# Rearranging the opening of a Fourier and mixture kernel on one NeuronCore: where mu is turned, who makes the angles, when the next butterflies run

## The chip, the cores and the metric

The kernel runs on one core of a Trainium2 chip. The metric is the device time of one execution in microseconds (us); medians are given with the lowest and highest run. The span, which the profile measures from the first to the last instruction, is about 1.8 us shorter.

## The reference, cut to what matters

```python
X = np.fft.fft(np.fft.fft(x, axis=1), axis=2).real          # x: 8 x 3072 x 256
x_prev = shifted by one row along the sequence, zero first
xk = mu_k * X + (1.0 - mu_k) * x_prev
xr = mu_r * X + (1.0 - mu_r) * x_prev
k = np.maximum(xk @ w_k, 0.0)                                # 256 -> 1024
v = k * k @ w_v                                              # 1024 -> 256
out = 1.0 / (1.0 + np.exp(-(xr @ w_r))) * v
```

## The kernel before

The transform is done by matmuls in stages. Stage A works on x (for later batches on sums and differences of its columns, the butterflies), stages D and C follow with tables of sines, and VectorE turns C's result `pq` into halves `y`, differences `d` and mixes `x`. Then come the K, V and R products of each of 48 chunks. The batches are interwoven: while the chunks of one batch are multiplied, the next batch is transformed. At the start there is nothing to interweave, so the opening is a chain. TensorE's products go to PSUM tiles `psW` and `psV`, and ScalarE or VectorE evacuates them.

```python
def mu_turn():                       # mu from a row onto the partitions, by TensorE
    ps = ps_v()
    for a in range(2):
        for i in range(2):
            nc.tensor.matmul(out=ps[:, c:c + 1], lhsT=mu_p[:, a, i], rhs=one, ...)
    V.tensor_copy(out=mu_f.rearrange("p a i -> p (a i)"), in_=ps[:, 0:4])
...
def loads():                         # all issued by GpSimd, in this order
    ... gathers of w_k ...
    nc.gpsimd.dma_start(out=wv_sb, in_=moe_w_v...)
    load_xh(1, 0)                    # x of batch 1, first half
    ... gathers of w_r ...
    load_xh(1, 1)                    # second half
...
    a_sum(0, 1, 4)                   # main sequence
    mu_turn()
    m_ends()                         # the end terms of the first table
    eo_rest()
    a_sum(0, 1, 8)
    a_sum(0, 1, 12, "V", 2)
    a_sum(0, 1, 14, "A", 2)
    m_angles(NS1, NSL)               # second table, on VectorE
    keep_busy(2)                     # two filler products on zeros
    d_half(0, 0, ps_v(), "A")
    ...
```

After that the work is put into numbered steps, one K step of a chunk each; `at(step, f, ...)` places it.

Of the kernel before, what the change touches and what calls it, by code (L numbers as in the profile page):

```python
# [9 lines left out]
FP32 = mybir.dt.float32  # L10
# [3 lines left out]
AF = mybir.ActivationFunctionType  # L14
ALU = mybir.AluOpType

TWO_PI = 2.0 * math.pi
MAGIC = 12582912.0


def _v(ap, extra_offset, free_dims):
    new_ap = [list(ap.ap[0])] + [[s, c] for (s, c) in free_dims]
    return dataclasses.replace(ap, offset=ap.offset + extra_offset, ap=new_ap)
# [12 lines left out]
def kernel(  # L36
# [10 lines left out]
    nc = tc.nc  # L47
# [3 lines left out]
    P = 128  # L51
    N1, R = 48, 64
    NSL = 27
    GU = 386
    NS1 = 17

    const = ctx.enter_context(tc.tile_pool(name="const", bufs=1))
# [16 lines left out]
    def ps_w():  # L74
        return ps_slot("W", 3, 1024)

    def ps_v():
        return ps_slot("V", 2, 512)
# [23 lines left out]
    def load_part(b, h, q0, nq):  # L102

        nc.gpsimd.dma_start(out=xh_t[b, h][:, q0:q0 + nq],  # L104
                            in_=x_r[b, :, 16 * h + q0:16 * h + q0 + nq, :])

    def load_xh(b, h):
        xh_t[b, h] = xh_pool.tile([96, 16, 256], FP16, name="xh")
        load_part(b, h, 0, 16)

    V = nc.vector
# [24 lines left out]
    def keep_busy(n):  # L136

        ps = ps_v()
        for _ in range(n):
            nc.tensor.matmul(out=ps[:, 0:512], lhsT=zeros[:, 0:P], rhs=zeros, start=True, stop=True)  # L140
# [14 lines left out]
                                 in_=_v(mu_row, f0, [(256, 2), (step, n)]), func=AF.Copy)  # L155

    def mu_turn():
        ps = ps_v()
        for a in range(2):
            for i in range(2):  # L160
                c = 2 * a + i
                nc.tensor.matmul(out=ps[:, c:c + 1], lhsT=mu_p[:, a, i], rhs=one,
                                 start=True, stop=True)
        V.tensor_copy(out=mu_f.rearrange("p a i -> p (a i)"), in_=ps[:, 0:4])
# [17 lines left out]
    for c in range(2):  # L182
        nc.gpsimd.tensor_scalar(out=ueo[:, :, c], in0=veo_i, scalar1=pd_f,
                                scalar2=(0.5 + 0.25 * c) * TURN, op0=ALU.mult, op1=ALU.add)
    load_part(0, 1, 0, 8)
    kst_i = const.tile([P, NSL + 64], INT32)
    nc.gpsimd.iota(kst_i[:, 0:NSL], pattern=[[1, NSL]], base=-1, channel_multiplier=0)
    nc.gpsimd.iota(kst_i[:, NSL:NSL + 64], pattern=[[1, 64]], base=0, channel_multiplier=0)
# [126 lines left out]
    def m_angles(s0, s1):  # L315
        V.tensor_tensor(out=ang[:, s0:s1], in0=_v(ast, s0, [(1, s1 - s0), (0, 64)]),
                        in1=_v(ast, NSL, [(0, s1 - s0), (1, 64)]), op=ALU.add)

    def m_wrap(s0, s1):
        V.tensor_scalar(out=ang[:, s0:s1], in0=ang[:, s0:s1], scalar1=TURN - 1,  # L320
                        scalar2=None, op0=ALU.bitwise_and)

    def m_sine(s0, s1):
        nc.scalar.activation(out=m1[:, s0:s1], in_=ang[:, s0:s1], func=AF.Sin, bias=m_pi,
                             scale=TWO_PI / TURN)
# [9 lines left out]
    def m_ends():  # L335


        for n, m in enumerate((m1, m2)):
            V.tensor_scalar(out=m[hi64, 0], in0=m[hi64, 0], scalar1=-1.0, scalar2=None,
                            op0=ALU.mult)  # L340
            V.tensor_copy(out=mz[lo64, n], in_=m[lo64, 1])
            V.memset(m[:, 0, 0:1], 0.0)

    def m_last():

# [18 lines left out]
    def loads():  # L364
        for a in range(2):
            next(row_part)
            gather(wk_sb[0][a], moe_w_k, a)
        nc.gpsimd.dma_start(out=wv_sb, in_=moe_w_v.rearrange("(fc p) v -> p fc v", p=128))
        load_xh(1, 0)
        for a in range(2):  # L370
            gather(wr_sb[0][a], moe_w_r, a)
        load_xh(1, 1)
        next(row_part)
        for a in range(2):
            gather(wk_sb[1][a], moe_w_k, 2 + a)
        for a in range(2):
            gather(wr_sb[1][a], moe_w_r, 2 + a)
# [92 lines left out]
    def c_item(b, s0, n, eng="A"):  # L470

        if s0 == 0:
            y_t[b] = y_pool.tile([P, 2, NSL, 64], FP16, name="y")
            y_t[b, "pq"] = y_pool.tile([P, 2, NSL, 64], FP16, name="pq")
        pq = y_t[b, "pq"]
        ps = ps_w()
        for i in range(n):
            sl = s0 + i
            u = {-1: 1, 24: 0, 25: 23}.get(sl - 1, sl - 1)
            for o, col, m, first, last in ((0, 128, m1, True, True), (512, 0, m2, True, b > 0),  # L480
                                           (512, 256, m1, False, True))[:2 if b else 3]:
                nc.tensor.matmul(out=ps[:, o + 64 * i:o + 64 * i + 64],  # L482
                                 lhsT=g_all[:, u, col:col + 128],
                                 rhs=m[:, sl] if sl != 1 else mz[:, 0 if m is m1 else 1],
                                 start=first, stop=last)
        if b and s0 + n == NSL:
            for k in range(2):
                nc.tensor.matmul(out=ps[:, 448:512], lhsT=u128[:, k],
                                 rhs=(m1, m2)[k][:, 1], start=(k == 0), stop=(k == 1))
        evac(pq[:, :, s0:s0 + n, :], _v(ps, 0, [(512, 2), (64, n), (1, 64)]), eng)  # L490
        if b and s0 + n == NSL:
            y_t[b, "f"] = f = y_pool.tile([NSL, 64], FP16, name="f")
            nc.scalar.activation(out=f, in_=ps[0:NSL, 448:512], func=AF.Copy)
# [16 lines left out]
    def halves(b, lo, hi, hs=(0, 1)):  # L510

        pq = y_t[b, "pq"]
        for h in hs:
            V.tensor_tensor(out=y_t[b][:, h, lo:hi], in0=pq[:, 0, lo:hi], in1=pq[:, 1, lo:hi],
                            op=ALU.subtract if h else ALU.add)

    def diff(b, lo, hi, hs=(0, 1)):
        if (lo, hs[0]) == (0, 0):
            x_t[b] = mix_pool.tile([P, 2, 26, 64], FP16, name="d")
        y = y_t[b]  # L520
        a0, a1 = hs[0], hs[-1] + 1
        V.tensor_tensor(out=x_t[b][:, a0:a1, lo:hi], in0=y[:, a0:a1, lo + 1:hi + 1],
                        in1=y[:, a0:a1, lo:hi], op=ALU.subtract)
# [65 lines left out]
                             in_=st["k", ds].rearrange("p (f t) -> p f t", f=2),  # L589
                             func=AF.Relu, bias=0.0, scale=0.25)  # L590

    def square(c, ds):
        r = st["rl"][:, 2 * ds - 2:2 * ds + 2]
        V.tensor_tensor(out=k2_t[c][:, 2 * ds - 2:2 * ds + 2], in0=r, in1=r, op=ALU.mult)  # L594

    def r_item(c):
        b, m, i = c
# [47 lines left out]
    m_swap(0, NS1)  # L645
    a_sum(0, 1, 0, "V")
    a_sum(0, 1, 4)
    mu_turn()
    m_ends()
    eo_rest()  # L650
    a_sum(0, 1, 8)
    a_sum(0, 1, 12, "V", 2)
    a_sum(0, 1, 14, "A", 2)
    m_angles(NS1, NSL)
    keep_busy(2)
    d_half(0, 0, ps_v(), "A")
    d_half(0, 2, ps_v(), "V")
    d_half(0, 4, ps_w(), "A")
    d_half(0, 6, ps_w(), "V")
    m_wrap(NS1, NSL)  # L660
    c_item(0, 0, 5)
    c_item(0, 5, 4)
    d_item(0, 2)
# [4 lines left out]
    work = {}  # L668

    def at(step, f, *args):  # L670
        work.setdefault((step, "x" if f in (a_item, a_sum, d_item, c_item, r_item, m_sine, d_pair) else "w"),
                        []).append((f, args))

    def mirrored_mu():

        for a in range(2):
            nc.gpsimd.tensor_copy(out=mu_m[:, a], in_=mu_f[:, 1 - a])
        nc.gpsimd.tensor_copy(out=mu_m[0:1], in_=mu_f[0:1])  # L678

    chunks = [(b, m, i) for b in range(B) for m in range(2) for i in range(3)]  # L680
    nk = 4 * len(chunks)
# [5 lines left out]
    for step, (c, tb) in v_steps.items():  # L687
        if c == chunks[-1] and tb >= 2:
            o_steps[step] = [(c, tb, 1)]
        elif tb % 2:  # L690
            o_steps[step + (step == LAG)] = [(c, tb, 2)]
    for lo, hi in ((0, 4), (4, 8)):
        halves(0, lo + (lo > 0), hi + 1)
        diff(0, lo, hi)
        mix_part(0, 0, lo, hi)
        if lo == 0:
            keep_busy(4)
            c_item(0, 9, 8)
            k_products(chunks[0], 0, 0, 256)
            k_products(chunks[0], 1, 0, 256)  # L700
    for n, c in enumerate(chunks):
        at(4 * n + (4, 5, 6)[(n < 3) + (n == 0)], r_item, c)


    at(0, halves, 0, 9, 17)
    at(1, m_sine, NS1, NSL)
    at(0, diff, 0, 8, 16)
    at(1, mix_part, 0, 0, 8, 16)
    at(2, m_swap, NS1, NSL)
    at(2, m_last)  # L710
    at(3, d_pair, 0, 16)
    at(4, d_item, 0, 5)
    at(4, mix_part, 0, 1, 0, 8)
    at(5, c_item, 0, 17, 8)
    at(5, halves, 0, 17, 25)
    at(5, diff, 0, 16, 24)
    at(5, mix_part, 0, 0, 16, 24)
    at(5, plain_128)
    at(5, mirrored_mu)
    at(6, a_sum, 1, 0, 0)  # L720
    at(6, a_sum, 1, 0, 4)
    at(6, mix_part, 0, 1, 8, 16)
    at(7, butterfly, 1, 1, 0)
    at(7, a_sum, 1, 0, 8)
    at(7, a_sum, 1, 0, 12)
    at(8, c_item, 0, 25, 2)
    at(8, load_xh, 2, 0)
    at(8, butterfly, 1, 1, 1)
    at(8, halves, 0, 25, 27)
    at(8, diff, 0, 24, 26)  # L730
    at(9, mix, 0, 0, 1, 0)
# [48 lines left out]
    for step in range(nk + LAG):  # L780
        if step < nk:
            k_piece(chunks[step // 4], step % 4)
        due(step, "x")
        v = v_steps.get(step)
        if v:
            v_tile(*v)
        due(step, "w")
        for v in o_steps.get(step, ()):
            v_out(*v)
        if step < nk and step % 2:  # L790
            square(chunks[step // 4], step % 4)
    assert not work, sorted(work)
    pin_order(first_inst)
# [30 lines left out]
```

## Time and profile before

| kernel before | time, us | span | clock granted | start of the third R item |
|---|---|---|---|---|
| three first runs | 460.49 (459.76 to 460.93) | | | |
| the profiled run that the prediction read | 458.33 | 456.6 | 0.997 | 50.36 |

The last column is a mark: the first R item of the third chunk, eight products of 128x256. TensorE has no long waits behind it. In every trace of this study the span minus this mark is 406.2 us. So whatever a version gains or loses has been gained or lost by then, and the mark can be compared from trace to trace.

### The profile page before, as it was taken

Reading aid. Unit: us, or ns where it says so; the run is one execution under the profiler, and the core shown is the slowest. Engines: PE = TensorE matmul, PEld = TensorE weight load, DVE = VectorE, ACT = ScalarE, POOL = GpSimd, SP = SyncE. Lnnn points to the kernel's source line nnn. Section 1 sums busy time; section 2 is a strip of 40 time slices with the busy share of each in tenths; the row PEclk is TensorE's granted clock in tenths of the full one; section 3 lists DMA queues with packets and bytes.
Section 4 is the critical chain, followed back from the end, with each engine's and each line's share of the span. In section 5 each row is a group of like instructions: output and inputs, shape, how many; then the busy total and the mean of one; then the engine's idle time right before and its main releaser. Section 6 shows DMA issues by size and latency. Waiting matters only on the chain.

```text
span 456.6 us, 9765 instructions
## 1 busy us (share of the span) xinstructions
PE 446.3 (98%) x4090; PEld 327.8 (72%) x4090; DVE 356.9 (78%) x497; ACT 360.6 (79%) x407; POOL 35.6 (8%) x71
## 2 busy tenths in 40 slices
PE   8989899999999999999999999999999999999995
PEld 5767677777777777777777777777777777666764
DVE  8878969986798778877789777888679755997453
ACT  7798898788878888888888888788878888666661
POOL 8828000000000000000000000000000000000000
PEclk9999999999999999999999999999999999999998
DMA  7983752626522373125712265221212121222223
GB/s 140 149 151 60 174 121 55 126 70 128 128 61 56 70 160 97 47 70 100 156 46 70 54 133 117 70 69 48 71 48 70 46 70 48 71 71 69 70 69 93
DMA packets 32300, 40.25 MB, mean 88 GB/s; under 512 B 3806, under 2 KB 29920, under 8 KB 30912
## 3 DMA queue, kind: packets, MB, share of 16 engines
q1 hardware_dynamic: 27776, 25.07, 22.0%
q0 software_dynamic: 4320, 14.42, 18.3%
q8 instruction: 32, 0.52, 0.5%
q10 hardware_dynamic: 160, 0.13, 0.1%
q14 instruction: 12, 0.10, 0.1%
HBM read 28.84 MB, written 25.17 MB: 118 GB/s over the span
## 4 chain that ended last, share of the span: by engine, by line
PE 89%; POOL 5%; DMA 2%; DVE 2%; issue 1%; POOLq 0%
PE psV L615 35%; PE psW L578 34%; PE psW L601 9%; PE psW L451 4%; PE psW L427 4%; PE psW L482 2%; DMA wr<-in_moe_w_r_dram,row_i 2%; POOL wk L359 1%; POOL wr L359 1%; POOL tw L400 1%; POOL m L351 1%; DVE x L547 0%; POOL row L290 0%; DVE t L534 0%; POOL w_eo L395 0%
## 5 line engine op out<-in xcount | busy, mean ns | idle before, releaser
L588 ACT ACTIVATE rl<-psW 128x1024 f16<-128x1024 f32 x192 | 196.6, 1025 | 81.4 <-PE psW L578 81.3
L615 PE MATMUL psV<-wv_sb,k 128*128 128x256 f16 x1536 | 198.8, 272 | 1.0 <-ACT g_all L415 0.8
L578 PE MATMUL psW<-x,wk 128*128 128x512 f16 (+1 forms) x776 | 196.9, 377 | 1.6 <-DVE x L547 1.2
L594 DVE TENSOR_TENSOR k<-rl 128x2048 f16<-128x2048 f16 x96 | 117.5, 1224 | 61.4 <-ACT rl L588 60.6
L615 PEld LDWEIGHTS <-k 128*128 128x128 f16 x1536 | 143.6, 98 | 21.3 <-issue 0.9
L578 PEld LDWEIGHTS <-wk 128*128 128x128 f16 x776 | 75.7, 98 | 51.5 <-issue 2.2
L625 DVE SCALAR_TENSOR_TENSOR o<-psV,r 128x512 f32<-128x512 f32 (+1 forms) x97 | 66.3, 684 | 23.7 <-PE psV L615 21.7
L547 DVE TENSOR_TENSOR x<-y,t 128x1536 f16<-128x1536 f16 x60 | 57.5, 959 | 2.1
L415 ACT ACTIVATE a<-psW 128x768 f16<-128x768 f32 x61 | 48.8, 806 | 2.8 <-PE psW L441 2.8
L601 PE MATMUL psW<-wr,x 128*128 128x256 f16 x384 | 49.8, 273 | 0.1
L606 ACT ACTIVATE r<-psW 128x1024 f16<-128x1024 f32 x48 | 49.0, 1020 | 0.8 <-PE psW L601 0.8
L601 PEld LDWEIGHTS <-x 128*128 128x128 f16 x384 | 37.6, 98 | 14.6 <-DVE k L594 0.4
L415 ACT ACTIVATE g_all<-psW 128x1024 f16<-128x1024 f32 (+1 forms) x46 | 46.9, 1025 | 0.0
L451 PEld LDWEIGHTS <-a 128*128 128x128 f16 x384 | 25.1, 98 | 10.3 <-issue 0.4
L427 PEld LDWEIGHTS <-eo 96*128 96x128 f16 x416 | 23.4, 97 | 11.6
L117 DVE TENSOR_TENSOR eo<-xh 96x2048 f16<-96x2048 f16 x26 | 31.6, 1215 | 0.0
L415 ACT ACTIVATE pq<-psW 128x896 f16<-128x896 f32 (+5 forms) x33 | 28.5, 868 | 0.9 <-PE psW L482 0.9
L451 PE MATMUL psW<-w_eo,a 128*128 128x128 f16 x368 | 27.7, 219 | 0.2 <-ACT rl L588 0.2
L104 POOL DMA_DIRECT2D xh<-in_x_dram x19 | 10.2, 540 | 225.6 <-DVE eo L117 224.5
L427 PE MATMUL psW<-w_pm,eo 96*128 96x96 f16 x416 | 26.3, 205 | 0.0
L482 PEld LDWEIGHTS <-g_all 128*128 128x128 f16 x459 | 17.8, 98 | 7.9 <-ACT g_all L415 1.1
L534 DVE TENSOR_SCALAR t<-d,mu_m 128x1536 f16<-128x1536 f16 x32 | 19.7, 615 | 1.8 <-POOL mu_m L678 1.8
(107 smaller groups left out, 171.9 us busy)
## 6 DMA issues: line engine op xcount, KB each, us to landing
out_dram<-o SPq DMA_DIRECT2D x190, 128.0 KB, 2.4
xh<-in_x_dram POOLq DMA_DIRECT2D x14, 768.0 KB, 6.8
xh<-in_x_dram POOLq DMA_DIRECT2D x3, 384.0 KB, 5.5
wv_sb<-in_moe_w_v_dram POOLq DMA_DIRECT2D x1, 512.0 KB, 8.5
xh<-in_x_dram POOLq DMA_DIRECT2D x2, 192.0 KB, 5.8
out_dram<-o ACTq DMA_DIRECT2D x2, 64.0 KB, 2.0
out_dram<-o SPq DMA_DIRECT2D x2, 64.0 KB
y<-f SPq DMA_DIRECT2D x7, 3.4 KB
```

The lines of the kernel that those rows point to most:

```text
L117: V.tensor_tensor(out=eo_t[b, h][:, :, e], in0=xh[:, :, 0:128], in1=xh[:, :, 128:256], op=ALU.subtract if e else ALU.add)
L415: nc.scalar.activation(out=out_ap, in_=in_ap, func=AF.Copy)
L427: nc.tensor.matmul(out=ps[:, 128 * i:128 * i + 96], lhsT=eo[:, 8 * j + i, e, :], rhs=w_pm[0:96, 0], start=True, stop=True)
L451: nc.tensor.matmul(out=_v(ps, 256 * i + 64 * (1 - e), [(128, 2), (1, 64)]), lhsT=a_t[b][:, e, 2 * u:2 * u + 2, :], rhs=w_eo[:, e, :], star ...
L547: V.tensor_tensor(out=dst, in0=_v(y_t[b], 64 * (NSL * a + lo + 3 * m), [(1, n)]), in1=_v(x_t["t", a], 64 * lo, [(1, n)]), op=ALU.subtract ...
L578: nc.tensor.matmul(out=st["k", ds][:, 512 * hs + lo:512 * hs + hi], lhsT=wk_sb[m][a][:, 128 * fc:128 * fc + 128], rhs=xk[:, a, 512 * i + l ...
L588: nc.scalar.activation(out=st["rl"][:, 2 * ds:2 * ds + 2], in_=st["k", ds].rearrange("p (f t) -> p f t", f=2), func=AF.Relu, bias=0.0, sca ...
L594: V.tensor_tensor(out=k2_t[c][:, 2 * ds - 2:2 * ds + 2], in0=r, in1=r, op=ALU.mult)
L601: nc.tensor.matmul(out=ps[:, 256 * tb:256 * tb + 256], lhsT=x_t[b, 1, m][:, a, 512 * i + 128 * tb: 512 * i + 128 * tb + 128], rhs=wr_sb[m] ...
L606: nc.scalar.activation(out=st["r", c], in_=ps, func=AF.Sigmoid)
L615: nc.tensor.matmul(out=st["v", tb - h][:, 256 * h:256 * h + 256], lhsT=k2_t[c][:, fc, 128 * tb:128 * tb + 128], rhs=wv_sb[:, fc], start=(f ...
L625: V.scalar_tensor_tensor(out=o.rearrange("p a b -> p (a b)")[:, 0:256 * n], in0=st["v", t0][:, 0:256 * n], scalar=16.0, in1=st["r", c][:, ...
```

## The change

Its intent: let the products that turn mu fill TensorE's wait behind stage A, take the second table's angles off VectorE, let the first chunk's squares start earlier, use VectorE's wait for stage C to do batch 1's butterflies, and keep GpSimd's preparations from holding up the mirrored mix. Cut to its core:

```diff
     def mu_turn():
-        ps = ps_v()
+        ps = ps_w()
...
-    load_part(0, 1, 0, 8)
+    load_part(0, 1, 0, 4)
+    load_part(0, 1, 4, 4)
...
+    def m_angles2():
+        g = nc.gpsimd
+        g.tensor_tensor(out=ang2[:, 0], ..., op=ALU.add)
+        g.tensor_scalar(out=ang2[:, 1], in0=ang2[:, 0], ..., op0=ALU.add, op1=ALU.subtract)
+        g.tensor_tensor(out=ang2[:, 0], in0=ang2[:, 0], in1=ang2[:, 1], op=ALU.subtract)
...
         nc.gpsimd.dma_start(out=wv_sb, in_=moe_w_v.rearrange("(fc p) v -> p fc v", p=128))
+        m_angles2()
         load_xh(1, 0)
...
-    mu_turn()
-    m_ends()
+    m_zero()
     eo_rest()
     a_sum(0, 1, 8)
     a_sum(0, 1, 12, "V", 2)
     a_sum(0, 1, 14, "A", 2)
-    m_angles(NS1, NSL)
-    keep_busy(2)
+    m_ends()
+    mu_turn()
...
-            nc.gpsimd.tensor_copy(out=mu_m[:, a], in_=mu_f[:, 1 - a])
+            V.tensor_copy(out=mu_m[:, a], in_=mu_f[:, 1 - a])
...
-    at(7, butterfly, 1, 1, 0)
-    at(8, butterfly, 1, 1, 1)
+    at(5, butterfly, 1, 1, 0)
+    at(5, butterfly, 1, 1, 1)
...
-        if step < nk and step % 2:
+        if step < 4:
+            square(chunks[0], step, 1)
+        elif step < nk and step % 2:
```

The cut leaves out smaller moves, among them that the first chunk's halves and differences now all run before its first mix.

More of the change, by code (lines that the diff above doesn't have):

```diff
@@ L321, in m_wrap, with m_sine2 @@
                         scalar2=None, op0=ALU.bitwise_and)
+    ang2 = const.tile([P, 2, NSL - NS1, 64], FP32)
+    def m_angles2():
+        g = nc.gpsimd
+        g.tensor_tensor(out=ang2[:, 0], in0=_v(ast, NS1, [(1, NSL - NS1), (0, 64)]),
+                        in1=_v(ast, NSL, [(0, NSL - NS1), (1, 64)]), op=ALU.add)
+        g.tensor_scalar(out=ang2[:, 1], in0=ang2[:, 0], scalar1=MAGIC * TURN,
+                        scalar2=MAGIC * TURN, op0=ALU.add, op1=ALU.subtract)
+        g.tensor_tensor(out=ang2[:, 0], in0=ang2[:, 0], in1=ang2[:, 1], op=ALU.subtract)
+    def m_sine2():
+        nc.scalar.activation(out=m1[:, NS1:NSL], in_=ang2[:, 0], func=AF.Sin, bias=0.0,
+                             scale=-TWO_PI / TURN)
     def m_sine(s0, s1):
@@ L340, in m_ends, with m_zero @@
                             op0=ALU.mult)
-            V.tensor_copy(out=mz[lo64, n], in_=m[lo64, 1])
             V.memset(m[:, 0, 0:1], 0.0)
+    def m_zero():
+        for n, m in enumerate((m1, m2)):
+            nc.scalar.activation(out=mz[lo64, n], in_=m[lo64, 1], func=AF.Copy)
     def m_last():
@@ L590, in k_piece, with square @@
                              func=AF.Relu, bias=0.0, scale=0.25)
-    def square(c, ds):
-        r = st["rl"][:, 2 * ds - 2:2 * ds + 2]
-        V.tensor_tensor(out=k2_t[c][:, 2 * ds - 2:2 * ds + 2], in0=r, in1=r, op=ALU.mult)
+    def square(c, ds, n=2):
+        lo, hi = 2 * ds + 2 - 2 * n, 2 * ds + 2
+        r = st["rl"][:, lo:hi]
+        V.tensor_tensor(out=k2_t[c][:, lo:hi], in0=r, in1=r, op=ALU.mult)
     def r_item(c):
@@ L659 @@
     d_half(0, 6, ps_w(), "V")
-    m_wrap(NS1, NSL)
     c_item(0, 0, 5)
@@ L670, in at @@
     def at(step, f, *args):
-        work.setdefault((step, "x" if f in (a_item, a_sum, d_item, c_item, r_item, m_sine, d_pair) else "w"),
+        work.setdefault((step, "x" if f in (a_item, a_sum, d_item, c_item, r_item, m_sine2) else "w"),
                         []).append((f, args))
@@ L676, in mirrored_mu @@
         for a in range(2):
-            nc.gpsimd.tensor_copy(out=mu_m[:, a], in_=mu_f[:, 1 - a])
-        nc.gpsimd.tensor_copy(out=mu_m[0:1], in_=mu_f[0:1])
+            V.tensor_copy(out=mu_m[:, a], in_=mu_f[:, 1 - a])
+        V.tensor_copy(out=mu_m[0:1], in_=mu_f[0:1])
     chunks = [(b, m, i) for b in range(B) for m in range(2) for i in range(3)]
@@ L691 @@
             o_steps[step + (step == LAG)] = [(c, tb, 2)]
+    halves(0, 0, 5)
+    halves(0, 5, 9)
+    diff(0, 0, 8)
     for lo, hi in ((0, 4), (4, 8)):
-        halves(0, lo + (lo > 0), hi + 1)
-        diff(0, lo, hi)
         mix_part(0, 0, lo, hi)
@@ L697 @@
             keep_busy(4)
-            c_item(0, 9, 8)
+            c_item(0, 9, 4)
+            c_item(0, 13, 4)
             k_products(chunks[0], 0, 0, 256)
@@ L705 @@
     at(0, halves, 0, 9, 17)
-    at(1, m_sine, NS1, NSL)
+    at(3, m_sine2)
     at(0, diff, 0, 8, 16)
-    at(1, mix_part, 0, 0, 8, 16)
-    at(2, m_swap, NS1, NSL)
-    at(2, m_last)
-    at(3, d_pair, 0, 16)
+    at(0, mix_part, 0, 0, 8, 16)
+    at(4, m_swap, NS1, NSL)
+    at(4, m_last)
+    at(4, d_item, 0, 4)
     at(4, d_item, 0, 5)
@@ L714 @@
     at(5, c_item, 0, 17, 8)
-    at(5, halves, 0, 17, 25)
-    at(5, diff, 0, 16, 24)
-    at(5, mix_part, 0, 0, 16, 24)
+    at(6, halves, 0, 17, 25)
+    at(6, diff, 0, 16, 24)
+    at(6, mix_part, 0, 0, 16, 24)
     at(5, plain_128)
     at(5, mirrored_mu)
-    at(6, a_sum, 1, 0, 0)
-    at(6, a_sum, 1, 0, 4)
-    at(6, mix_part, 0, 1, 8, 16)
-    at(7, butterfly, 1, 1, 0)
+    at(5, a_sum, 1, 0, 0)
+    at(7, a_sum, 1, 0, 4)
+    at(5, mix_part, 0, 1, 8, 16)
+    at(5, butterfly, 1, 1, 0)
     at(7, a_sum, 1, 0, 8)
-    at(7, a_sum, 1, 0, 12)
+    at(8, a_sum, 1, 0, 12)
     at(8, c_item, 0, 25, 2)
     at(8, load_xh, 2, 0)
-    at(8, butterfly, 1, 1, 1)
+    at(5, butterfly, 1, 1, 1)
     at(8, halves, 0, 25, 27)
```

## The prediction

> **What bounds the kernel now.** I read the page first, then busy time by stretch, then the timeline of the opening, then the waits and the chain of its first 52 us.
>
> ```profile
> PE 446.3 (98%) x4090; PEld 327.8 (72%) x4090; DVE 356.9 (78%) x497; ACT 360.6 (79%) x407; POOL 35.6 (8%) x71
> ...
> PE 89%; POOL 5%; DMA 2%; DVE 2%; issue 1%; POOLq 0%
> ```
>
> The chain that ended last is TensorE for 89% of the span, 406 us. What is not TensorE (POOL, DMA, DVE, issue: 10%) lies in the first 48 us: the listed pieces of the chain before 44 us are GpSimd and one transfer, and those after 48 us are TensorE. The 98% hides this, for it adds overlapping durations: one 128x256 product shows 272 ns, but the chain gives eight in 0.87 us, 109 ns each. So I counted work, not busy time, before 47.6 us. From the timeline's start-to-start times: eight stage-A products 0.65 us (64 of batch 0: 5.2), stages D and C some 3.2 and 3.5, twelve K steps, eight V tiles and two R items at 0.87 (19.1), batch 1's A products 3.7. That is 35 us. Of the other 12.6, six are the lead-in: the first A product starts at 5.99, when x lands. **At most about 6.6 us can be had**, 1.4% of the whole.
>
> ```profile
> 20.00:25.00 5.00, 4.90 (x37) 3.04 (x35) 4.68 (x8) 4.59 (x6) 3.94 (x4) 1.00 1.12 212
> 25.00:30.00 5.00, 3.97 (x51) 2.95 (x51) 3.37 (x6) 4.99 (x8) 0.00 (x0) 1.00 1.03 203
> 45.00:50.00 5.00, 3.78 (x39) 2.71 (x37) 4.97 (x7) 3.25 (x4) 0.00 (x0) 1.00 0.98 187
> 60.00:100.00 40.00, 40.00 (x398) 29.90 (x396) 34.24 (x46) 34.40 (x41) 0.51 (x1) 1.00 0.42 91
> ```
>
> Columns: stretch, length, busy us of PE, PEld, DVE, ACT, POOL, then clock, DMA share, GB/s. From 20 to 30 us the loads fill the DMA engines, ScalarE is busy 9.6 of 10 us and TensorE waits. Past 60 us TensorE never idles; what is gained or lost before stays in the total, and nothing later adds to it.
>
> **The change, part by part, against the timeline.**
>
> ```profile
> 11.17 1.05 PE L162 MATMUL psV<-one,mu_p 1*128 1x1 f32 x8
> ...
> 13.99 0.61 POOL L104 DMA_DIRECT2D xh<-in_x_dram  x1
> ...
> 14.19 0.59 PE L140 MATMUL psV<-zeros 128*128 128x512 f16 x2 [0.55 <-DVE a L413]
> 14.62 0.61 PE L451 MATMUL psV<-w_eo,a 128*128 128x128 f16 x8
> ...
> 17.19 0.58 POOL L104 DMA_DIRECT2D xh<-in_x_dram  x1
> ...
> 30.72 0.76 DVE L514 TENSOR_TENSOR y<-pq 128x512 f16<-128x512 f16 x2 [2.21 <-ACT pq L415]
> ...
> 33.45 2.93 POOL L351 TENSOR_SCALAR m<-m 64x64 f16<-64x64 f16 x4 [8.60 <-DMA wr<-in_moe_w_r_dram,row_i]
> ...
> 43.31 0.62 DVE L534 TENSOR_SCALAR t<-d,mu_m 128x1536 f16<-128x1536 f16 x1 [1.84 <-POOL mu_m L678]
> ...
> 47.63 0.81 PE L578 MATMUL psW<-x,wk 128*128 128x512 f16 x3 [1.22 <-DVE x L547]
> ```
>
> 1. *Turning mu.* Its products stand inside stage A for 1.05 us. Moved behind A, they fill the 0.55 us wait for A's last evacuation, and two filler products (0.59 us) go. Stage A then follows x: the last part seems to land near 12.1 us, its eight products take 0.65, the turning products run to 13.6 beside the evacuation (13.4). D starts near 13.75 instead of 14.62: **0.9 us**, carried through D and C to the first K products. The sixth part of x (one more 0.55 us issue) lets half a part start 0.4 us sooner, but the transfers set the end of A; this is inside the 0.9.
> 2. *Second table.* VectorE loses 0.82 + 0.48 us of angles; GpSimd gains two tensor-tensors and a tensor-scalar on 128x640 fp32[...]. They stand between the load of w_v and the first x load of batch 1, so that issue slips from 14.0 to about 18.5 us.
> 3. *Squares of the first chunk in four pieces.* VectorE has the second half at 27.18 now (25.95 + 1.23). In four pieces of 0.61 behind the second mix (22.8) they end near 25.1. V's first tile, in two bits at 26.46 and 27.23 now, runs near 25. The step of stage D that held V's banks goes to the other ones. With step 1, ScalarE's run of evacuations to the C evacuation (29.67 + 1.02 = 30.7) ends near 29.8, and the A products of batch 1, one pulled forward, leave the seventh step about **1.7 us** early.
> 4. *Butterflies of batch 1 in the C wait.* VectorE has 2.21 us free there. Two butterflies are 2 x 1.21 = 2.42 us, but they need batch 1's second half. It was issued at 17.19; the longest of the x loads took 13.5 us, so it landed at 30.7, the moment the wait now ends. In the new order VectorE's 1.41 us mix and the mu copies end near 29, it stops for x, then runs the butterflies, a square (1.22), halves (0.76), differences (0.69) and mix (1.42), on which the third chunk's K products wait. If x lands at 31.2: 31.2 + 2.42 + 1.22 + 0.76 + 0.69 + 1.42 = 37.7. Those products start at 37.65 now; TensorE would be ready for them near 35.5 (1.7 sooner, and one A item of 0.65 now stands behind them). **The lead of step 3 is spent here.**
> 5. *Exchanged mu on VectorE.* Takes away the 1.84 us wait at 43.31. GpSimd's preparations no longer hold the mirrored x, which TensorE waited 1.22 us for before the product at 47.63. New chain on VectorE: mix 37.7, two outputs 1.36, square 1.22, halves and differences 0.67 with their wait, one mirrored half (0.62 + 0.96), a square 1.22, the other half: 46. TensorE from 37.7: K 0.87, the displaced A item 0.65, C 0.26, K and R 1.74, A 0.35, V 0.87, then K, A, V twice at 2.09: 46.6. So it doesn't wait, and the mirrored K step ends at 46.6 + 0.87 = 47.5 where it ends at 48.3 now (the next A item starts at 48.28). **About 0.9 us are left over at that point, from all parts together**, and TensorE is full from there on. Copying mz on ScalarE, and fewer VectorE instructions there, cost nothing on the path.
>
> [...] a one-element GpSimd tensor-scalar at 6.86 us took 1.28 us beside a 1.29 us VectorE add, its neighbour 0.28. [...] This trace has no such instruction; its 128-element tensor-scalar took 0.37, the one-element one 0.22, which makes about 1.0 for 640. [...] x of batch 1, issued at 14 us, landed 11.2 us later. [...]
>
> **Rivals.** *A, the load is late.* The x load slipping 4.5 us could move its landing. For it: the engines run dry at 12.8 to 14.2 us already, for lack of issues. Against: w_v landed at 21.5 (13.04 + 8.5), so the engines had it to do until about 20.5, and 18.5 plus the 0.9 us from first issue to first traffic is 19.4. I take 0.5 us of slip. With 2 us instead, the chain of step 4 starts the K products at 39.2, and the total is 39.2 - 37.7 - 0.9 = 0.6 us slower: 461.1. *B[...].* The angles lie at 14.4 to 18.5 us, where VectorE's halves and differences begin (near 16.2). [...] the first mix is late by about a microsecond: 460.5, the gain gone. For it: the 1.28 us above[...]; against:[...] VectorE's own times stayed at 1.22 to 1.26 us beside GpSimd's work at 33 to 36 us. *C, the x is there in time.* If x landed under 29 us, step 3's lead would hold and with the 1.2 us wait gone the total would be near 457.8. Against: the DMA engines moved 203 GB/s at full share to 30 us. *D, late constants.* GpSimd's end-of-table work waited for the last gather to 33.45 us; as late as 34, it ends at 37.3, before C's last part needs it near 39. It becomes a stall only where rival A's slip is large.
>
> **Time, range and chances.** 460.5 − 0.9 = 459.6. A or B take up to 1.5 us more than that; C gives 2 us. The three runs before span 1.2 us. I put the range at 457.7 to 461.4. Two per cent is 9.2 us, more than the 6.6 us that are in the opening; slower by as much would need several of these stalls. Faster 0.02, same 0.97, slower 0.01.
>
> **What would show each step.** Right: D's first product near 13.75; [...]V's first tile near 25; a VectorE wait for a transfer of x of about 2 us before the first butterfly, ending near 31.2; a TensorE wait of about 2 us for the mix ahead of the third chunk; none for the mirrored mix. Wrong: butterflies before 30 us (C); halves stretched or waiting beside GpSimd before 18 us (B); x at 32 us or later (A); and any change of spacing past 60 us, which nothing here explains.

The forecast for the second table's three GpSimd instructions came to about 4 us, a sum of three terms; only the 1.0 us for the tensor-scalar is worked out from the trace. So the 18.5 us for the end of the angles and the issue of x was the author's estimate and not shown, and the landing at 31.2 leans on it. Of rival B, what the trace shows is the 1.28 us of a one-element GpSimd instruction beside VectorE's 1.29, and the microsecond by which the first mix would be late was an estimate. In rival A the 0.9 us from first issue to first traffic is SyncE's first load (0.75 to 1.67 us); for the first load of x it is 1.36 (1.26 to 2.62). And in the trace the DMA engines are nearly idle from 12.8 to 13.7 us, not to 14.2.

## The result, and the profile after

| | median, us | lowest to highest | runs |
|---|---|---|---|
| before, same rounds | 460.28 | 459.76 to 460.93 | 6 |
| changed | 458.99 | 458.84 to 459.26 | 6 |

The ratio is 0.9973, with a 95% interval of 0.996 to 0.9985: within 2%, and 1.3 us faster by the medians. A ratio here is the mean time of one kernel's fast runs over that of the other's of the same rounds (in the later rounds without the run that was profiled), so it is not quite the ratio of the medians. All of the changed kernel's six runs lie within 0.42 us.

The page of the changed kernel's profiled run (459.26 us, span 457.5) shows the same balance as before: busy time of the engines, then shares of the chain that ended last.

```profile
PE 449.0 (98%) x4088; PEld 329.9 (72%) x4088; DVE 359.2 (79%) x497; ACT 361.2 (79%) x409; POOL 40.8 (9%) x72
...
PE 90%; POOL 4%; DMA 2%; DVE 1%; issue 1%; ACT 0%; POOLq 0%
```

GpSimd has gained 5.2 us of work, about what the angles take (5.27). Busy time by stretch, with the columns explained in the prediction:

```profile
20.00:25.00 5.00, 4.85 (x49) 3.13 (x48) 4.09 (x10) 3.20 (x5) 4.26 (x6) 0.92 0.95 134
45.00:50.00 5.00, 5.00 (x55) 3.75 (x53) 4.97 (x7) 4.04 (x5) 0.81 (x2) 1.00 0.86 152
60.00:100.00 40.00, 40.00 (x396) 29.92 (x395) 33.47 (x46) 34.40 (x41) 0.51 (x1) 1.00 0.41 90
```

Three things differ. From 20 to 25 us the loads moved 134 GB/s where they moved 212 before: the two halves of batch 1's x were issued at 19.87 and 23.18 us instead of 13.99 and 17.19. From 45 to 50 us TensorE no longer idles. And the clock of the first row is 0.92: it was at 0.50 from 13.96 to 20.79 us, for 6.83 us. In the openings the stretches at 0.50 are 3.41, 6.83 or 13.65 us long; what sets them off was not shown. Past 60 us nothing changed.

The timeline of the opening (start, length, engine, line, operation; in brackets the idle time before and what ended it):

```profile
13.08 1.40 DVE L355 TENSOR_SCALAR m<-m 64x64 f16<-64x64 f16 x1
13.48 0.99 POOL L387 DMA_DIRECT2D wv_sb<-in_moe_w_v_dram  x1
13.69 0.82 PE L471 MATMUL psV<-w_eo,a 128*128 128x128 f16 x8
14.47 1.31 POOL L329 TENSOR_TENSOR ang<-ast 128x640 f32<-128x640 f32 x1
14.62 1.21 DVE L355 TENSOR_SCALAR m<-m 64x64 f16<-64x64 f16 x1
15.87 2.38 POOL L331 TENSOR_SCALAR ang<-ang 128x640 f32<-128x640 f32 x1
15.88 0.16 DVE L164 COPY mu_f<-psW 128x4 f32<-128x4 f32 x1
16.09 0.32 PE L502 MATMUL psW<-m,g_all 128*128 128x64 f16 x3 [0.72 <-DVE mu_f L164]
17.96 2.31 DVE L534 TENSOR_TENSOR y<-pq 128x320 f16<-128x320 f16 x4 [0.73 <-ACT pq L435]
18.34 1.58 POOL L333 TENSOR_TENSOR ang<-ang 128x640 f32<-128x640 f32 x1
19.87 0.60 POOL L104 DMA_DIRECT2D xh<-in_x_dram  x1
28.01 1.27 PE L636 MATMUL psV<-wv_sb,k 128*128 128x256 f16 x8
48.35 1.03 PE L598 MATMUL psW<-x,wk 128*128 128x512 f16 x4
51.29 1.04 PE L622 MATMUL psW<-wr,x 128*128 128x256 f16 x8
```

In the first trace of the kernel before, an end term and C's start were:

```profile
12.45 0.18 DVE L339 TENSOR_SCALAR m<-m 64x64 f16<-64x64 f16 x1
15.70 0.26 PE L482 MATMUL psW<-m,g_all 128*128 128x64 f16 x3
```

Stage D starts at 13.69 instead of 14.62, so the first step worked. Then it is lost: two end-term instructions of VectorE (L355, on 64x64) take 1.40 and 1.21 us where one took 0.18 before. They lie beside GpSimd's issue of w_v and its first angle instruction, and end with these (14.48 and 14.47, 15.83 and 15.78). Behind them stands the copy of mu out of PSUM, so C starts at 16.09. Before, C started at 15.70. A second loss follows. VectorE's four halves (L534) take 2.31 us, where the same four took 1.04 before, in two pairs. The trace, instruction by instruction, has three of them at 0.28 to 0.33 us and one of 128x256 at 1.57, from 18.50 to 20.07, beside GpSimd's third angle instruction (18.34 to 19.92). From C's start to the first K product it is 5.57 us (16.09 to 21.66); before it was 4.15 (15.70 to 19.85).

The chain that ended last, in order of time (start, length, what), takes up the other end of the story:

```profile
19.87 0.60 POOL xh L104
...
23.18 9.68 DMA xh<-in_x_dram
...
32.88 2.35 DVE eo L117 x2
35.24 1.14 DVE k L615
36.38 0.72 DVE y L534 x2
...
37.12 0.70 DVE d L542
...
37.85 1.43 DVE x L578 x2
...
39.32 0.82 PE psW L598 x3
```

The angles hold back the x loads, the second half lands at 32.86, and from there VectorE's butterflies and mix lead to TensorE's third chunk at 39.32. Before, those products started at 37.65. The load alone cost little in this trace: VectorE's mix before the butterflies ended only at 32.63, so VectorE waited 0.25 us for x.

So the trace of the changed kernel is 0.9 us **later** at the mark than the trace that the prediction read (51.29 against 50.36), and yet the timed runs are 1.3 us faster. The experiments had to explain that first.

### The profile page after: what moved, and what is told of

Read it like the earlier page. It is cut to its first block, busy times and chain, and to the rows that moved or that the text cites. A ratio compares the mean times of both kernels' runs of the same rounds, so it can differ in the third digit from the quotient of the medians.

```text
span 457.5 us, 9763 instructions
## 1 busy us (share of the span) xinstructions
PE 449.0 (98%) x4088; PEld 329.9 (72%) x4088; DVE 359.2 (79%) x497; ACT 361.2 (79%) x409; POOL 40.8 (9%) x72
## 4 chain that ended last, share of the span: by engine, by line
PE 90%; POOL 4%; DMA 2%; DVE 1%; issue 1%; ACT 0%; POOLq 0%
PE psV L636 36%; PE psW L598 35%; PE psW L622 9%; PE psW L471 4%; PE psW L447 4%; PE psW L502 2%; DMA xh<-in_x_dram 2%; POOL xh L104 1%; POOL ang L331 1%; DVE eo L117 1%; POOL wk L378 0%; POOL wr L378 0%; POOL ang L333 0%; DVE x L578 0%; POOL ang L329 0%
## 5 line engine op out<-in xcount | busy, mean ns | idle before, releaser
L615 DVE TENSOR_TENSOR k<-rl 128x2048 f16<-128x2048 f16 (+1 forms) x98 | 117.5, 1202 | 61.5 <-ACT rl L608 60.7
L471 PEld LDWEIGHTS <-a 128*128 128x128 f16 x384 | 26.3, 101 | 9.5
L471 PE MATMUL psW<-w_eo,a 128*128 128x128 f16 x376 | 29.5, 225 | 0.0
L502 PEld LDWEIGHTS <-g_all 128*128 128x128 f16 x459 | 18.5, 100 | 8.4 <-issue 1.3
L534 DVE TENSOR_TENSOR y<-pq 128x896 f16<-128x896 f16 (+5 forms) x38 | 19.9, 566 | 2.6 <-ACT pq L435 2.6
```

The costliest lines, as they stand in the source:

```text
L471: nc.tensor.matmul(out=_v(ps, 256 * i + 64 * (1 - e), [(128, 2), (1, 64)]), lhsT=a_t[b][:, e, 2 * u:2 * u + 2, :], rhs=w_eo[:, e, :], star ...
L615: V.tensor_tensor(out=k2_t[c][:, lo:hi], in0=r, in1=r, op=ALU.mult)
```

## The experiments

Twelve experiments ran, each in five rounds; all gave correct results. Kernels are compared only within the same rounds. "After" below is the changed kernel.

### 1. The kernel before, once more

No edit.

> The kernel before, unchanged. Open: its profiled run took 458.3 us (mean clock 0.997) and its six timed ones 460.3 in the median, 2 us more. Theory 'two clocks': the opening of the kernel before runs in some executions at a granted clock of 0.50 for a few us, as the changed kernel's profiled run does from 14.0 to 20.7 us, and the run that was first profiled missed it. Then the runs here have mean clocks near 0.993 to 0.995 where they take 460 us, and a new trace shows a stretch at 0.50 before 30 us. Rival 'the timed runs have a fixed addition': the trace again spans 456.6 at full clock in the opening, and the timed runs are 460 us all the same. Ratio to itself 1.000 in either.

Median 460.51 us (459.98 to 461.56); before in these rounds 460.96 (459.75 to 462.93); ratio 0.9993, 0.9971 to 1.0015. The profiled run took 461.37 us. Its mark stands at 53.33 us, 3 us later than in the first trace. In every trace the span minus this mark is 406.2 us. The timeline of TensorE and ScalarE in this trace:

```profile
21.98 0.52 PE L482 MATMUL psW<-m,g_all 128*128 128x64 f16 x12 [0.39 <-ACT g_all L415]
24.29 1.02 ACT L415 ACTIVATE pq<-psW 128x1024 f16<-128x1024 f32 x1 [2.37 <-PE psW L578]
25.36 0.81 PE L578 MATMUL psW<-x,wk 128*128 128x512 f16 x3 [1.04 <-ACT pq L415]
53.33 1.04 PE L601 MATMUL psW<-wr,x 128*128 128x256 f16 x8
```

C's last product is done at 22.50 by its record, but ScalarE takes it up at 24.29. The packed trace also holds the semaphore updates, which the views don't print. In the first trace every update of TensorE's semaphore stands within 30 ns of the recorded end of its product. Here the update for C's last product stands at 24.27, 1.77 us behind, and the next two are late by 1.89 and 1.50. Together with late x parts (stage A waited 1.21 and 0.36 us for them) and one stretch at half clock, from 15.38 to 18.80 us, this sets the trace apart; how much of the 3 us each of them makes up was not separated. The expected explanation by the clock alone fails: three of the six runs had a mean clock of 1.000 and still took 459.98 to 460.17 us. **The first trace of before was an unusually good run:** no other run of this kernel in the first comparison or on three of the four chips was under 459.5 us; on the fourth (experiments 5 to 8) three of eleven took 458.12 to 458.34. Late updates turned up in nine of the thirteen traces after the first: in the changed kernel's own, in all eight experiments on three of the chips, and in none of the four (5 to 8) on the remaining one. There the kernel before is faster, too (median 459.28, against 460.13 to 460.96 on the three others). They all come before 33 us. Why they are late stays open. The profile gives the ends of products as modelled, so the trace alone can't say whether a product or its update was late. In one trace (experiment 10) three updates came at 18.11, 18.20 and 18.29, though eight products stood between each and the next, which take 0.45 us; that speaks for late updates rather than late products, in that one trace.

### 2. Part 1 undone in the changed kernel

```diff
-        ps = ps_w()
+        ps = ps_v()
...
     a_sum(0, 1, 4)
+    mu_turn()
     m_zero()
...
     m_ends()
-    mu_turn()
+    keep_busy(2)
```

> The changed kernel with the turning products and the two filler products back where they were (part 1 undone). Theory 'clock': [...] with them back the clock stays at 1.00 there, C and the first K products come some 2 us sooner in the trace, total 457.5 to 458.5 against 459.0 of the changed kernel. Rival 'part 1 is worth its 0.9 us': total 459.5 to 460, D's first product near 14.6 instead of 13.7, and the clock falls all the same[...].

Median 460.09 us (459.21 to 465.5), ratio 1.0001, 0.9959 to 1.0044. Two of the six runs took 465.0 and 465.5 us with a mean clock of 0.985 and 0.984, and the profiled one is the first of them: its clock was at 0.50 for 13.65 us. No run reached the 457.5 to 458.5 of the clock theory, but with such a clock the trace can't test it. The four others lie between 459.21 and 460.28. They are 0.2 to 1.3 us above the changed kernel's median, which fits the predicted size without proving it, for the changed kernel ran on another chip.

### 3. Part 2 undone: the angles back on VectorE

```diff
         nc.gpsimd.dma_start(out=wv_sb, in_=moe_w_v.rearrange("(fc p) v -> p fc v", p=128))
-        m_angles2()
         load_xh(1, 0)
...
     a_sum(0, 1, 14, "A", 2)
+    m_angles(NS1, NSL)
     m_ends()
...
     d_half(0, 6, ps_w(), "V")
+    m_wrap(NS1, NSL)
...
-    at(3, m_sine2)
+    at(3, m_sine, NS1, NSL)
```

> The changed kernel with the second table's angles back on VectorE (part 2 undone). Theory [...] the two sign changes take 0.2 instead of 1.2 to 1.4 us, C starts near 14.9 instead of 16.1, x of batch 1 is issued near 14.5 and 17.7 instead of 19.9 and 23.2, and the butterflies start at 31 instead of 32.9: total 457 to 458. Rival [...]: 459 or more, with C no sooner than 15.7.

Median 459.65 us (457.97 to 464.81), ratio 0.999, 0.9948 to 1.0032: outside the expected 457 to 458, and the interval is too wide to say more. The trace does: C starts at 15.01, the butterflies at 31.51 without a wait for a load, and the third chunk at 38.71 without waiting for the mix. The first end term still ends with the issue of w_v (14.44 and 14.43; it takes 0.42 us), the second takes 0.18: so the first wait comes from the place of the end terms, the second from the angles. Both waits of the changed kernel further on, for x and for the mix, are gone, but the mark, at 50.96, is hardly earlier, for late updates (0.82 and 1.05 us behind at two parts of C), for which ScalarE had to wait, took their place.

### 4. The end terms ahead of the last sums, all else as after

```diff
     m_zero()
+    m_ends()
     eo_rest()
...
-    m_ends()
     mu_turn()
```

> The changed kernel with the end terms (four VectorE instructions) moved ahead, to about 11.8 us, before GpSimd issues w_v or starts the angles; nothing else. Theory [...]: the C start at 16.1 us is the wait for these and for nothing else; it comes to about 15.0, TensorE's gap of 0.7 us goes[...]; x of batch 1 still lands at 32.9, so the third chunk still starts at 39.3 and the total stays within 0.3 of 459.0 us. Rival 'the gap and the clock bind the total': 457 to 458.

Median 459.04 us (458.51 to 459.74), ratio **0.9962**, 0.9942 to 0.9983. VectorE's timeline:

```profile
12.10 0.18 DVE L355 TENSOR_SCALAR m<-m 64x64 f16<-64x64 f16 x1
13.78 0.16 DVE L164 COPY mu_f<-psW 128x4 f32<-128x4 f32 x1 [0.23 <-PE psW L162]
18.16 2.96 DVE L578 SCALAR_TENSOR_TENSOR x<-d,mu_f,y 128x256 f16<-128x256 f16 x4
32.09 2.35 DVE L117 TENSOR_TENSOR eo<-xh 96x2048 f16<-96x2048 f16 x2 [1.92 <-DMA xh<-in_x_dram]
```

Away from GpSimd's work the end term takes 0.18 us again, mu is there at 13.78, and C starts at 14.78, as the prediction had it (about 14.8). The halves take 1.18 us. But the four first mixes now lie beside the third angle instruction (18.32, 1.72 us) and take 2.96 us instead of 1.67; TensorE waits 1.17 us for them. And now the DMA wait that the prediction expected before the butterflies is there in full: 1.92 us, until 32.09. So VectorE loses time beside GpSimd's angles (rival B) in either order, 1.27 us at the halves after the change and 1.29 at the mixes here, and the late x catches what is left.

### 5. Part 4 undone: butterflies back at steps 7 and 8

```diff
-    at(5, butterfly, 1, 1, 0)
+    at(7, butterfly, 1, 1, 0)
...
-    at(5, butterfly, 1, 1, 1)
+    at(8, butterfly, 1, 1, 1)
```

> The changed kernel with the two butterflies of batch 1 back at their old places (part 4 undone); everything else stays. Theory 'pinned by x': in the changed kernel the third chunk's K products wait for the load of x, issued at 23.2 us behind GpSimd's angles and landed at 32.9, by way of butterflies 2.35, square, halves, differences, mix. With the butterflies later the mix is ready near 36.7 and the K products start when TensorE is free, near 38.5: 0.3 to 1 us is gained, total 458.0 to 458.7 against 459.0, and the runs spread more with the clock, for nothing hides it any longer. Rival 'the C wait is the better place': later butterflies delay A items or VectorE's mirrored mix, total 459.5 to 460.5.

Median 458.61 us (458.44 to 459.12); before in these rounds, on another chip, 459.28 (458.12 to 462.44); ratio 0.9987, 0.996 to 1.0013. TensorE starts the third chunk at 38.41 and doesn't wait for the mix. Among the three undo experiments of these rounds this is the fastest, by 0.4 us, and its trace shows the stop for x gone. Their runs overlap, and the changed kernel did not run on this chip: that the move into the C wait does not pay where x is late is likely, but not shown by the times.

### 6. Part 5 undone: exchanged mu back on GpSimd

```diff
-            V.tensor_copy(out=mu_m[:, a], in_=mu_f[:, 1 - a])
-        V.tensor_copy(out=mu_m[0:1], in_=mu_f[0:1])
+            nc.gpsimd.tensor_copy(out=mu_m[:, a], in_=mu_f[:, 1 - a])
+        nc.gpsimd.tensor_copy(out=mu_m[0:1], in_=mu_f[0:1])
```

> The changed kernel with the exchanged mu copied on GpSimd again (part 5 undone). Theory 'GpSimd's preparations would bind now': they end at 44.6 us in the changed kernel's trace, 1.3 us after VectorE takes the first mirrored half (42.9); with the copies behind them VectorE waits about 2.2 us, the mirrored K products start near 49.6 instead of 48.35, total 460.0 to 460.4. Rival 'the mirrored mix has slack': total 458.8 to 459.3 and no wait of TensorE before the mirrored chunk.

Median 458.98 us (458.49 to 459.27), ratio 0.9991, 0.9964 to 1.0018. VectorE waits again:

```profile
43.82 0.62 DVE L554 TENSOR_SCALAR t<-d,mu_m 128x1536 f16<-128x1536 f16 x1 [1.27 <-POOL mu_m L697]
```

TensorE does not wait, because it comes to the mirrored product at 48.01, later than in the trace the prediction read, and VectorE has the slack. Part 5 took away a wait that was on the path in that trace and is not in this order. Without late updates the load of x shows: VectorE waits for it 1.25 us here, until 32.52, and 0.95 us in experiment 7.

### 7. Part 3 undone: squares in two pieces

```diff
-        if step < 4:
-            square(chunks[0], step, 1)
-        elif step < nk and step % 2:
+        if step < nk and step % 2:
             square(chunks[step // 4], step % 4)
```

> The changed kernel with the first chunk's squares in two pieces of 2048 again (part 3 undone). Theory 'no effect': in the changed kernel's trace all four pieces stand back to back behind the mix that ends at 26.4 us, so they start late for VectorE and not for want of their inputs; two pieces end at the same 28.8 us, total 458.8 to 459.3. Rival 'V's first tile starts by pieces and that shortens the path': V's first tile goes from 28.0 to 28.7 or later, total 459.5 or more.

Median 459.42 us (458.57 to 460.45), ratio 1.0002, 0.9973 to 1.0031. V's first tile runs in two bits again, at 27.48 and 28.30, with a wait of 0.22 us for the square. Compared with the other undo experiments of these rounds part 3 may be worth some 0.4 us; the interval doesn't settle it.

### 8. Both repairs together: end terms early, angles on VectorE

The edits of experiments 3 and 4 in one kernel.

> The changed kernel with the angles back on VectorE and the end terms moved ahead (the edits of the two runs before, together). Theory: no GpSimd instruction but DMA issues and index sums is left before 34 us[...], and x of batch 1 lands near 31.5 as with the angles back; C starts near 15.0, first K products near 19.5, third chunk's K products near 38.0, total 457.0 to 458.0 with full clock. Rival 'run-to-run clock and landing times decide': no clear difference from the end terms alone, 458.5 to 459.5, with a wider spread than the changed kernel's.

Median **457.07 us** (456.7 to 460.05), against 459.28 of before in the same rounds; ratio 0.9964, 0.9931 to 0.9997. C starts at 15.11, the butterflies at 30.02 after 0.75 us of DMA wait, the third chunk at 36.40 and the mark at 48.65, the earliest of all. The trace has no late update and full clock. The halves take their old time:

```profile
16.55 1.02 DVE L533 TENSOR_TENSOR y<-pq 128x320 f16<-128x320 f16 x4 [0.18 <-ACT pq L434]
```

From C's start to the first K product (19.26) it is 4.15 us again. The traces of experiments 5 to 7, from the same chip and without late updates too, have the halves at 2.31 to 2.33 us, V's first tile at 27.48 to 27.56 (here 25.04), the landing of x at 31.34 to 32.96 (here 30.00) and the mark at 50.60 to 51.41. Half clock isn't what sets them apart: experiment 7 has none in its opening. **The place of the angles and of the end terms costs about 2 us at the mark, where nothing else hides it** (one trace each; the medians are 458.61 to 459.42 against 457.07).

### 9. Part 1 alone, on the kernel before

```diff
-        ps = ps_v()
+        ps = ps_w()
...
-    mu_turn()
     m_ends()
...
-    keep_busy(2)
+    mu_turn()
```

> Part 1 alone on the kernel before: the products that turn mu go behind stage A in place of the two fillers; the second table's angles stay on VectorE, nothing goes to GpSimd, and the end terms stay before the last sums[...]. Theory (part 1 is worth what the prediction gave it, 0.9 us at D's start, where TensorE's own chain sets the end, as in the repeat of the kernel before): D's first product near 13.8, median 0.5 to 0.9 us under the kernel before of the same rounds, and the gain shrinks to nothing in any run whose end is set by GpSimd's chain to the mirrored mu. Rival [...]: D's first product near 13.8 but a window of 0.50 of clock in the opening and no faster than before.

Median 459.56 us (458.5 to 464.14); before on this chip 460.24 with the slow run (fast runs 459.56 to 464.2); ratio 0.9991, 0.9945 to 1.0037. D's first product starts at 13.82 and C at 14.89 (14.62 and 15.70 before). The medians differ by 0.7 us, as expected, but one run of 464.14 makes the interval wide. The clock was full throughout, so in this trace the missing fillers cost none of it. After 15 us late updates took the lead away again: the updates for the two parts of C, due at 16.16 and 20.73, came at 17.69 and 21.72.

### 10. The combined kernel on a further chip

> The combined kernel (end terms ahead of the last sums, angles of the second table back on VectorE), unchanged, on a further chip. It was 457.07 with an interval of 0.9931 to 0.9997 of before, wide because its before runs spread. Theory (it takes away both costs of the move to GpSimd[...]): 1.5 to 3 us under the kernel before of the same rounds, the DMA wait ahead of the butterflies under 1 us, no wait for the third chunk's mix. Rival (the earlier result was a lucky set of clocks): within 1 us of the changed kernel's 459.

Median 459.64 us (458.9 to 461.61), ratio 0.9984, 0.9949 to 1.0019: **the expectation failed**. ScalarE's timeline, first of experiment 8, then of this one, shows why:

```profile
15.81 1.19 ACT L434 ACTIVATE pq<-psW 128x640 f16<-128x640 f32 x2 [0.27 <-PE psW L501]
18.72 1.35 ACT L434 ACTIVATE pq<-psW 128x512 f16<-128x512 f32 x2
```

```profile
15.95 0.70 ACT L434 ACTIVATE pq<-psW 128x640 f16<-128x640 f32 x1 [0.27 <-PE psW L501]
18.13 0.60 ACT L434 ACTIVATE pq<-psW 128x512 f16<-128x512 f32 x1 [1.47 <-PE psW L470]
```

Up to 15.95 us the two traces are the same but for 0.14 us. Then the second piece of `pq` waits 1.47 us: its product's record ends at 16.51, its update came at 18.11. TensorE runs dry for 1.44 us, and one stretch at half clock follows, from 20.92 to 24.33 us. The mark is at 51.95, 3.3 us later, with the same instructions in the same order.

### 11. The combined kernel with the butterflies back

The edits of experiments 8 and 5.

> The combined kernel with the butterflies of batch 1 back at steps 7 and 8. Theory (with x early, they stand in the C wait without cost, and putting them back costs what VectorE must then do between the sums): same as the combined kernel or up to 0.5 us slower, no DMA wait ahead of the second table's mixes. Rival (VectorE's stop for x costs even here): 0.3 to 0.8 us faster than the combined kernel.

Median 459.31 us (458.01 to 459.99), ratio 0.997, 0.9937 to 1.0003. It is 0.3 us below the combined kernel of the same chip, too little for these intervals. The trace has the same late update at C (due 16.07, come 17.34).

### 12. The changed kernel once more

> The changed kernel, unchanged, on a further chip. Theory (its opening ends with the x load of batch 1, which neither the clock of the opening nor late signals of TensorE move): its fast runs again within about 0.6 us of each other, near 459, while the kernel before of the same rounds spreads over 2 us or more; butterflies again start with a DMA wait, at 32.5 to 33.2 us. Rival (the narrow spread of the first six runs was chance): a spread like that of the kernel before.

Median 459.31 us (458.91 to 459.77); before 460.13 (459.58 to 461.09); ratio **0.9981**, 0.9969 to 0.9993. The gain holds. The fast runs lie within 0.86 us, before within 1.51: narrower, but by less than expected. The butterflies start at 32.54 without a DMA wait, as the mix before them ends, so in this run the load was not what held them. What repeated to the hundredth is the other end:

```profile
12.87 1.61 DVE L355 TENSOR_SCALAR m<-m 64x64 f16<-64x64 f16 x1
14.63 1.21 DVE L355 TENSOR_SCALAR m<-m 64x64 f16<-64x64 f16 x1
```

D was even earlier here (13.48), but mu's copy starts at 15.88 and C at 16.09, as in the first trace, for the second end term (14.63, 1.21 us) again ends beside GpSimd's first angle instruction (14.47, 1.31 us). The halves take 2.31 us here too, one of them 1.57. Put together, C starts at 15.94 to 16.09 us in the five traces where the end terms lie beside the angles (after, its repeat, experiments 5, 6 and 7), and at 14.78 to 15.25 in the six where they do not (3, 4, 8 to 11). Experiment 2 is left out: at its half clock stage A itself was late.

## Why the prediction was right or wrong

**The number was right, in part by luck.** Predicted 459.6, measured 458.99 and, in the repeat, 459.31; the predicted gain was 0.9 us, the medians show 1.3 and 0.8. But the step "460.5 − 0.9" took a median of typical runs and subtracted a gain worked out on a trace of 458.33 us. In that trace GpSimd's late constants and the mirrored mix set the end. In the one trace of a typical run (experiment 1) late updates of TensorE's semaphore (1.50 to 1.89 us), late x parts (1.21 and 0.36) and a stretch of 3.41 us at half clock delay it, and TensorE doesn't wait for the mirrored mix. The sum hit because losses that were underrated stood against a start that was too good: taken from its own trace it gives 458.33 − 0.9 = 457.4, and the changed kernel's profiled run took 459.26. At the mark the change costs 0.9 us against that trace.

- **Turning mu (0.9 us).** Right at D: 13.69 for a predicted 13.75, 13.82 in experiment 9. "Carried through D and C" failed: C starts 0.39 us later than before, as the end terms (1.40 and 1.21 us for 0.18 before) and mu's copy end only with GpSimd's instructions. Experiment 4 gives it back, with C at 14.78.
- **Second table (4 us).** Mis-sized and mis-split: 1.31, 2.38 and 1.58 us, and 5.40 from the first start to the x issue at 19.87 instead of 18.5. In the seven traces that have them it is 1.31 to 1.32, 2.38 to 2.39 and 1.54 to 1.72. The tensor-scalar, 1.0 in the estimate, is the dearest.
- **Rival B, VectorE beside GpSimd.** The loss came, twice; by what mechanism was not shown. First at the end terms, which the prediction had not looked at (C 1.1 to 1.3 us later than in experiments 3 and 4). They are lengthened beside a mere DMA issue, too: the first took 1.40 and 1.61 us (after and its repeat) and 0.42 in experiment 3, without any angles, and each time ended with the issue of w_v; in experiment 1 one that started 0.43 us after that issue took 0.56 and ended with it, while those that started within 0.03 us of its start took 0.18 (before and experiment 1). Then at the halves, where it had put it: one took 1.56 to 1.63 us instead of 0.28 to 0.33 in all five traces of the changed order, and the first K product starts at 21.66, 5.57 us behind C, instead of 4.15. The argument against it misread its lines: from 33 to 36 us VectorE indeed kept its 1.26, but GpSimd's four instructions there took 0.46, 1.07, 0.57 and 0.60 us, so one of them took nearly twice as long as the others.
- **Squares (V's first tile near 25, lead 1.7 us).** Wrong: 28.01. The squares could not start earlier, because C, halves, mixes and K before them were late. In experiment 8, with the end terms early and the angles on VectorE, V starts at 25.04, in experiments 5 to 7 on the same chip at 27.48 to 27.56: the step was right for a chain that the second step had broken.
- **Butterflies.** The mechanism was right: x, butterflies, square, halves, differences, mix and K form the chain, as the trace shows link by link. Two terms were mis-sized, and K came at 39.32 for 37.7. One is the landing, 32.86 for 31.2, which is what rival A had (32.7). The other is VectorE's mix before the butterflies, which ended at 32.63 where the prediction had it near 29. So the waits of about 2 us were 0.25 and 0.17; the first is 1.25 and 0.95 in experiments 6 and 7, without late updates, and 1.92 with the end terms early (experiment 4).
- **Exchanged mu.** TensorE indeed no longer waits for the mirrored mix, but starts it at 48.35 instead of the predicted 46.6. In experiment 6 undoing the part brings no wait of TensorE back, and the time doesn't change by more than the noise. Two sums of the prediction are off without changing a conclusion: the VectorE pieces listed from 37.7 add up to 45.3 us, not 46, and the squares' 22.8 and four times 0.61 make 25.2, not 25.1.
- **Late constants (rival D).** GpSimd's end-of-table work could start only at 35.66 (the rival's own case was 34), but C's last part came late as well, at 40.63, and did not wait.

**Where the gain over a typical run comes from** is shown only in outline. At D the change is 0.9 us ahead. Its opening contains time lost to GpSimd's neighbourhood (C 0.39 us later than before, the halves 1.27 longer) and to the load (0.25), in which a late update or a stretch of low clock can hide, so it suffers less from them; that is argued, from the narrower spread, and not shown. On the chip without late updates the three near variants were at 0.9987 to 1.0002 of before, which fits, but the changed kernel itself was not run there. **A version that beats both:** the combined kernel did by 2.2 us of medians on one chip and by 0.6 on another, where the interval includes no gain. Whether it beats the changed kernel in general stays open.

## What to carry to other kernels

Before working out a gain on a trace, compare that run's time with the median: a trace that is better than typical can have another critical path, as here that of 458.33 us had against a median of 460.49. Work moved to an idle GpSimd was not free here: count what is queued behind it, here the loads (issued at 19.87 instead of 13.99 us), and which VectorE instructions lie beside it (halves of 2.31 us instead of 1.04). A lead is worth only what the next wait leaves of it, here nothing of the 0.9 us at D, as C started 0.39 us later; so follow each saved microsecond to the mark behind which nothing waits.
